# Projected keys copied out once, and their rows placed by transfers on chip

## The chip, the core and the metric

The kernel runs on one core of one Trainium2 chip. Its five engines each follow their own instruction list: TensorE (PE, matrix products; its weight loads are listed as PEld), VectorE (DVE), ScalarE (ACT), GpSimd (POOL) and SyncE (SP, which here issues nearly all transfers). [...]

The metric is the device time of one execution in microseconds. Three runs of the kernel before gave 834.16, 834.82 and 836.92 us; the median is 834.82 us.

## The reference, cut to what matters

One transformer block on 2048 tokens of width 512: adaptive layer norm, attention with 32 heads of 16 columns each, and a gated feed-forward part with 1792 inner columns.

```python
h = _layernorm(x) * (1 + ca) + sa
q, k, v = (h @ wqkv) split into 32 heads of 16
p = softmax(q @ k.T * 16 ** -0.5)        # per head, 2048 x 2048
x = x + ga * ((p @ v) @ wo)
h = _layernorm(x) * (1 + cb) + sb
x = x + gb * ((gelu(h @ w_gate) * (h @ w_up)) @ w_down)
```

The exponentials of the softmax are 32 x 2048 x 2048 numbers. The kernel handles them as 2048 tiles of 128 x 512.

## The kernel before, in words

**Heads and key buffers.** A block `dc` of 128 projected columns holds eight heads of 16 rows. The kernel works on four heads at a time, a head quad `qd` from 0 to 7: block `dc = qd // 2`, and in it the even heads (`ee = 0`) or the odd ones (`ee = 1`). Each of the four products of a quad takes a strip of 32 partitions, `32*j` to `32*j + 31`, which holds one even and one odd head. So that the product sees only one of the two, keys are stored twice: `km[0]` (`kme` in the profile) has the rows of the odd heads set to zero, and `km[1]` (`kmo`) those of the even heads. `side_k` makes them for one key group `g` of 512 tokens and one block `dc`: four products into the PSUM bank `mi`, then two VectorE instructions, each of which multiplies the whole bank by a column of zeros and ones (`self.rm`) and writes one of the two buffers.

**The stream of score tiles.** `stream()` goes through all tiles in order of position: quads 0 and 1 of the first 512 queries interleaved, then quads 2, 3 and on. For each step `qk()` puts two or three score tiles into one half of six PSUM banks, and one ScalarE instruction takes their exponential (line 336). Some rounds of four tiles are given to VectorE instead: four instructions turn scores into bits (line 348, `mreg<-ps_sc` and `dreg<-ps_sc`), and three more (`power_task`, lines 348 and 340) split and square them. Such a round is here called a vector round; it needs two free 2048-column buffers, keys and values that are marked as there, and a VectorE that the planner holds to be free soon.

**Who sets the order.** Nothing is scheduled at run time. While the program is built, `rec()` keeps a modelled clock for every engine and takes the next piece of work greedily: a score step, a product with values, a piece of side work, a vector round. What comes out is one fixed list per engine. `rec()` also finds each instruction's waits from the bytes that it reads and writes. One rule of it matters here: a transfer always waits, on its issuing engine, for the one before it on the same semaphore.

```python
if dma is not None and seq > 1:
    needs[stream] = seq - 1
```

The planner charges a transfer 450 ns of SP, and lets it land no earlier than 1.9 us after its issue began; the two masked key instructions are charged 661 ns each and a plain copy of the same bank 601 ns.

**Side work.** Projections for later quads are side work, spread over positions by `plan()`. `side_first` makes block 0 for key groups 1 to 3. Then `side_wo_load` clears `wo` on VectorE, waits until that is recorded, and issues eight transfers of 64 KB (`wo<-in_A_wo_dram`). After it come `side_dc(1)`, `side_mod`, `side_dc(2)`, `side_q_all(1)`, `side_dc(3)`; each `side_dc` makes the queries of a block and then, for the four key groups in turn, `side_k` and `side_v`. All share the one bank `mi`. As soon as the last product of `side_k` is planned, its key is marked as there (`self.done(("k", g, dc))`), and score steps and vector rounds may use it; the products then wait at their semaphores.

**What else SP issues.** After the loads of the prologue and `wo`, each finished quad gives a chain of eight transfers through DRAM for its softmax denominators (`unit_end`: `scr_den<-osb`, `den<-scr_den`, `scr_rec<-rden`, four times `rb<-scr_rec`). `rb` holds the reciprocals; GpSimd sets it to zero in the prologue, and until the last positions only rows `32*j` to `32*j + 15` of it are written.

## Time and profile before

| | |
|---|---|
| median of three runs | 834.82 us |
| the profiled execution: time, span | 834.12 us, 832.4 us |
| granted TensorE clock, mean | 0.994 |
| ACT busy | 799.0 us (96%) |
| PE busy | 744.3 us (89%) |
| DVE busy | 740.1 us (89%) |
| POOL busy | 4.5 us (1%) |
| score instructions on ScalarE | 716, 754.6 us |
| score tiles on VectorE | 400 (272 into `mreg`, 128 into `dreg`) |
| masked key instructions in `side_k` | 15 into `kme`, 15 into `kmo` |

The profiled execution is the program once, taken by the hardware profiler. Its span runs from the first to the last instruction; the remaining 1.7 us of its time lie around that. An engine that is busy 96% of the span is not thereby the bound in every stage, so the busy times are read by stage, and the chain of work that ended last is followed back. In the rows, `L318` is the line of the helper that records all matrix products, `L336` that of ScalarE instructions, `L348`, `L357` and `L340` those of the VectorE helpers, and `L386` that of transfers; the names behind the line (`kme<-ps_mi,rm`) tell the pieces apart. `SPq` is SP's queue issuing a transfer.

### The profile page before, as it was taken

The page shows a single profiled execution, that of the slowest core. Times are in us where ns is not written, and L with a number is a line of the kernel's source. Part 1 is how long each engine was busy: PE and PEld are TensorE (multiplying, and loading weights), DVE is VectorE, ACT ScalarE, POOL GpSimd, SP SyncE. Part 2 cuts the span into 40 slices and gives each one's busy share as a digit, 9 for nine tenths or more (in the row PEclk, how much of TensorE's full clock was granted, in tenths as well). Part 3 has the DMA queues.
Part 4 walks back from the last instruction along what each step waited for, and adds up shares of the span by engine and source line. Part 5 has one row for each costly group of instructions (what it writes and reads, how often), then busy time and mean ns, then how long its engine had stood idle before and what let it go on. Part 6 is the DMA issues. An engine that isn't in the chain of part 4 may idle for free.

```text
span 832.4 us, 29218 instructions
## 1 busy us (share of the span) xinstructions
PE 744.3 (89%) x13207; PEld 289.5 (35%) x13207; DVE 740.1 (89%) x1330; ACT 799.0 (96%) x754; POOL 4.5 (1%) x12
## 2 busy tenths in 40 slices
PE   8888989888898988899998989998889889898988
PEld 3333332322222221222333333333443344345556
DVE  7857999999999998999999999979999999597664
ACT  5999999999999999999999999999999999999982
POOL 2000000000000000000000000000000000000000
PEclk9999999999999999999999999999999999999999
DMA  9100000000003211110003212102462432500000
GB/s 287 43 23 16 9 10 9 10 9 8 9 9 90 59 46 34 46 34 22 23 6 96 64 48 56 54 26 59 139 182 62 135 93 70 152 13 7 20 7 13
DMA packets 76358, 43.68 MB, mean 52 GB/s; under 512 B 20557, under 2 KB 74634, under 8 KB 76234
## 3 DMA queue, kind: packets, MB, share of 16 engines
q1 hardware_dynamic: 76232, 41.82, 17.8%
q8 instruction: 103, 1.69, 0.8%
q14 instruction: 21, 0.17, 0.1%
q10 hardware_dynamic: 2, 0.00, 0.0%
HBM read 39.18 MB, written 2.61 MB: 50 GB/s over the span
## 4 chain that ended last, share of the span: by engine, by line
ACT 69%; PE 15%; DVE 10%; DMA 3%; SPq 1%; issue 1%; DVEq 0%
ACT E L336 66%; PE ps_sc L318 7%; PE ps_mi L318 6%; DVE mreg L348 3%; ACT hreg L336 2%; PE ps_pv L318 2%; DMA scr_rec<-rden 2%; DVE dreg L348 1%; SPq L386 1%; DMA rb<-scr_rec 1%; ACT L336 1%; DVE dreg L340 1%; DVE mreg L340 1%; DVE onorm L340 1%; DVE st L376 0%
## 5 line engine op out<-in xcount | busy, mean ns | idle before, releaser
L336 ACT ACTIVATE E<-ps_sc 128x1024 bf16<-128x1024 f32 (+2 forms) x716 | 754.6, 1263 | 19.0 <-PE ps_sc L318 18.6
L318 PE MATMUL ps_sc<-qT,kmo 32*128 32x256 bf16 (+2 forms) x1664 | 196.8, 299 | 23.6 <-ACT E L336 22.1
L318 PE MATMUL ps_sc<-qT,kme 32*128 32x256 bf16 (+2 forms) x1600 | 193.0, 306 | 25.2 <-ACT E L336 22.1
L348 DVE TENSOR_SCALAR mreg<-ps_sc 128x512 uint16<-128x512 f32 x272 | 182.3, 684 | 15.7 <-PE ps_sc L318 13.1
L318 PE MATMUL ps_pv<-E,vaug 128*17 128x256 bf16 (+2 forms) x2576 | 151.4, 300 | 2.2 <-DVE osb L357 1.5
L318 PE MATMUL ps_mi<-wreg,mreg 128*32 128x256 bf16 (+1 forms) x1856 | 108.4, 331 | 7.9 <-DVE hreg L340 3.1
L318 PEld LDWEIGHTS ps_sc<-qT,kme 32*128 32x128 bf16 x1600 | 53.1, 92 | 144.3 <-ACT E L336 119.1
L318 PEld LDWEIGHTS ps_sc<-qT,kmo 32*128 32x128 bf16 x1664 | 55.3, 92 | 130.4 <-ACT E L336 110.1
L348 DVE TENSOR_SCALAR dreg<-ps_sc 128x512 uint16<-128x512 f32 x128 | 85.8, 685 | 11.5 <-PE ps_sc L318 10.7
L318 PEld LDWEIGHTS ps_pv<-E,vaug 128*17 128x17 bf16 x2576 | 52.8, 89 | 58.9 <-issue 41.5
L348 DVE TENSOR_SCALAR mreg<-mreg 128x2048 uint16<-128x2048 uint16 x99 | 67.0, 682 | 0.2
L318 PEld LDWEIGHTS ps_mi<-wreg,mreg 128*32 128x32 bf16 x1856 | 41.5, 96 | 49.7 <-issue 21.0
L318 PE MATMUL ps_pv<-mreg,vaug 128*17 128x256 bf16 (+2 forms) x740 | 44.4, 304 | 5.9 <-DVE mreg L340 3.6
L340 DVE TENSOR_TENSOR dreg<-mreg,dreg 128x2048 bf16<-128x2048 bf16 x37 | 44.8, 1212 | 0.0
L318 PE MATMUL ps_mi<-hreg,wreg 128*32 128x512 bf16 x480 | 39.4, 385 | 1.3 <-DVE vaug L357 0.6
L340 DVE TENSOR_TENSOR mreg<-mreg 128x2048 bf16<-128x2048 bf16 x31 | 37.5, 1211 | 0.1
L340 DVE TENSOR_TENSOR hreg<-ps_mi,hreg 128x512 bf16<-128x512 f32 x46 | 31.5, 685 | 5.0 <-PE ps_mi L318 4.8
L357 DVE CAST hreg<-ps_mi 128x512 bf16<-128x512 f32 x46 | 31.5, 684 | 1.4 <-PE ps_mi L318 1.3
L318 PE MATMUL ps_pv<-dreg,vaug 128*17 128x256 bf16 (+2 forms) x508 | 31.1, 303 | 1.8 <-DVE dreg L340 1.4
L318 PE MATMUL ps_mi<-wo,onorm 128*32 128x512 bf16 x416 | 32.3, 384 | 0.1
L348 DVE TENSOR_SCALAR dreg<-dreg 128x2048 uint16<-128x2048 uint16 x44 | 30.0, 682 | 0.0
L318 PE MATMUL ps_mi<-mreg,hreg 128*32 128x512 bf16 x352 | 28.6, 384 | 0.0
(160 smaller groups left out, 668.4 us busy)
## 6 DMA issues: line engine op xcount, KB each, us to landing
mreg<-in_B_w_up_dram SPq DMA_DIRECT2D x32, 256.0 KB, 2.9
mreg<-in_B_w_gate_dram SPq DMA_DIRECT2D x28, 256.0 KB, 3.6
mreg<-in_B_w_down_dram SPq DMA_DIRECT2D x16, 256.0 KB, 2.7
dreg<-in_B_w_down_dram SPq DMA_DIRECT2D x12, 256.0 KB, 5.0
mreg<-in_w_mod_dram SPq DMA_DIRECT2D x1, 2048.0 KB, 12.1
rb<-scr_rec SPq DMA_DIRECT2D x64, 32.0 KB, 1.8
out_dram<-xs SPq DMA_DIRECT2D x16, 128.0 KB, 1.7
rb<-scr_rec SPq DMA_DIRECT2D x116, 16.0 KB, 1.7
```

The source lines that it names most:

```text
L318: return self.rec("pe", lambda e: e.matmul(out, lhsT, rhs, start=start, stop=stop, tile_position=tp), [lhsT, rhs, *after], [out], cost=(n, ...
L336: return self.rec("act", lambda e: e.activation(out, in_, func, scale=scale, **kw), rd, wr, cost=self.cost("act", out, [in_], "act") + load)
L340: return self.rec(eng, lambda e: e.tensor_tensor(out, a, b, op), [a, b], [out], cost=self.cost(eng, out, [a, b], "tt"))
L348: return self.rec(eng, lambda e: e.tensor_scalar(out, a, s1, s2, **kw), rd, [out], cost=self.cost(eng, out, [a], "ts") + (60 if len(rd) > ...
L357: return self.rec(eng, lambda e: e.tensor_copy(out, in_), [in_], [out], cost=self.cost(eng, out, [in_], "ts"))
L386: return e.dma_start(out, in_)
```

## The change

For block 0 nothing changes. For blocks 1 to 3 `side_k` copies the bank once, without a mask, into a new staging buffer `kst` (two halves, taken in turn by key groups), and then issues eight transfers from SP, one for each strip `j` and each of even and odd: 16 rows of 512 bf16, from `kst` into the rows of that head in `kme` or `kmo`. The rows of the other heads have to be zero, so a new function `zero_rows` issues 24 transfers, of 16 rows by 2048 columns, from rows of `rb` that stay zero into those rows of `kme` and `kmo`. It is called in `side_wo_load`, ahead of the loads of `wo`. The zero rows and the key rows of one strip in one of the two buffers share one semaphore, `dk0` to `dk7`.

```diff
@@ alloc
+        self.kst = sb("kst", [P, 2, 512], BF16)
@@ side_k
         def fin(mi):
-            self.ts("dve", self.km[0][:, dc, sl], mi, self.rm[:, 0:1], None, ALU.mult)
-            self.ts("dve", self.km[1][:, dc, sl], mi, self.rm[:, 1:2], None, ALU.mult)
+            if dc == 0:
+                self.ts("dve", self.km[0][:, dc, sl], mi, self.rm[:, 0:1], None, ALU.mult)
+                self.ts("dve", self.km[1][:, dc, sl], mi, self.rm[:, 1:2], None, ALU.mult)
+            else:
+                st = self.kst[:, g % 2, :]
+                self.copy("dve", st, mi)
+                for j in range(4):
+                    for ee in range(2):
+                        r = slice(32 * j + DH * ee, 32 * j + DH * ee + DH)
+                        self.dma("sp", self.km[ee][r, dc, sl], st[r, :], "dk%d" % (2 * j + ee))
             self.done(("k", g, dc))
         yield from self.side_proj(512 + P * dc, g, fin)
+
+    def zero_rows(self):
+
+        z = self.rb[:, :].bitcast(BF16)
+        for j in range(4):
+            for ee in range(2):
+                r = 32 * j + DH * (1 - ee)
+                for dc in range(1, NDC):
+                    self.dma("sp", self.km[ee][r:r + DH, dc, :], z[32 * j + DH:32 * j + 2 * DH, :], "dk%d" % (2 * j + ee))
@@ side_wo_load
         yield from self.until("wo0")
+        if not self.dry:
+            self.zero_rows()
         selv = self.self32[:, :].rearrange("p (a b) -> p a b", b=32)
```

## The prediction

> **What bounds the kernel now.** I read the page's busy times first, then the chain of work that ended last between 40 and 130 us, then the busy times by stretch.

> ```profile
> span 832.4 us, 29218 instructions
> PE 744.3 (89%) x13207; PEld 289.5 (35%) x13207; DVE 740.1 (89%) x1330; ACT 799.0 (96%) x754; POOL 4.5 (1%) x12
> ...
> 44.47 85.81 ACT E L336 x80
> ...
> core 0: us, PE busy (x) PEld busy (x) DVE busy (x) ACT busy (x) POOL busy (x), PEclk, DMA share, GB/s
> 55.00:85.00 30.00, 27.33 (x536) 10.19 (x532) 23.01 (x45) 30.00 (x29) 0.31 (x1) 1.00 0.11 26
> 85.00:165.00 80.00, 71.61 (x1286) 25.06 (x1282) 77.93 (x126) 80.00 (x76) 0.00 (x0) 1.00 0.04 10
> 165.00:330.00 165.00, 144.04 (x1724) 39.64 (x1724) 159.30 (x258) 163.87 (x153) 0.00 (x0) 0.99 0.12 33
> 700.00:832.00 132.00, 118.92 (x2607) 64.47 (x2603) 88.01 (x179) 111.91 (x115) 0.00 (x0) 0.99 0.14 35
> ```

> From 44.5 us on ScalarE does exponentials without a gap: 85.81 us of the chain are one piece of 80 instructions. The end therefore moves only in two ways: by the number of tiles that ScalarE has to do, or by a gap that it is given. VectorE takes tiles off it, and from 85 to 165 us it is itself full (77.93 of 80). From 55 to 85 us it isn't (23.01 of 30): there the first vector rounds wait for keys and values, not for VectorE.

> **The masked pair against the copy.** Twelve key evictions change, those of blocks 1 to 3. Of these, four lie in 55:85 and eight in 85:165.

> ```profile
> L348 DVE TENSOR_SCALAR kme<-ps_mi,rm 128x512 bf16<-128x512 f32 x15 | 11.2, 748 | 6.1 <-PE ps_mi L318 6.1
> L348 DVE TENSOR_SCALAR kmo<-ps_mi,rm 128x512 bf16<-128x512 f32 x15 | 11.1, 743 | 0.0
> ...
> 95.58 0.75 DVE L348 TENSOR_SCALAR kme<-ps_mi,rm 128x512 bf16<-128x512 f32 x1
> 96.25 0.74 DVE L348 TENSOR_SCALAR kmo<-ps_mi,rm 128x512 bf16<-128x512 f32 x1
> 96.91 1.42 DVE L340 TENSOR_TENSOR wo<-wo,ga 128x512 bf16<-128x512 bf16 x4
> 98.46 0.69 DVE L357 CAST vaug<-ps_mi 128x512 bf16<-128x512 f32 x1
> 99.07 0.68 DVE L348 TENSOR_SCALAR mreg<-ps_sc 128x512 uint16<-128x512 f32 x1
> ...
> 104.54 0.68 DVE L348 TENSOR_SCALAR mreg<-mreg 128x2048 uint16<-128x2048 uint16 x1
> 105.14 0.69 DVE L348 TENSOR_SCALAR dreg<-dreg 128x2048 uint16<-128x2048 uint16 x1
> ...
> 107.35 1.22 DVE L340 TENSOR_TENSOR mreg<-mreg 128x2048 bf16<-128x2048 bf16 x1
> 108.48 0.69 DVE L348 TENSOR_SCALAR mreg<-ps_sc 128x512 uint16<-128x512 f32 x1
> ...
> L336 ACT ACTIVATE E<-ps_sc 128x1024 bf16<-128x1024 f32 x47 | 46.0, 1164 | 0.0
> L336 ACT ACTIVATE E<-ps_sc 128x1536 bf16<-128x1536 f32 x29 | 41.6, 1576 | 0.0
> ```

> Durations overlap on VectorE, so I count from start to start. The pair takes 96.91 - 95.58 = 1.33 us. The nearest row to the copy, same bank and same output type, is the cast of `vaug`: 99.07 - 98.46 = 0.61. Saved: 0.72 us per eviction, 5.8 us for the eight where VectorE is full, 8.6 us for all twelve.

> What VectorE does with it: a vector round is four tiles at about 0.61 (the same pitch), two bit operations at 0.60 (105.14 - 104.54) and a square at 1.13 (108.48 - 107.35), 4.77 us or 1.19 per tile. ScalarE did 47 x 2 + 29 x 3 = 181 tiles in these 80 us, 0.44 per tile. When both are full, n tiles more on VectorE shorten the time by 0.44 n and fill 5.8 = (0.44 + 1.19) n, so n = 3.6 and the gain is 1.6 us. With all twelve it is 5.3 tiles and 2.3 us; with none taken, 0. I take 1.6, since only the full stretch turns time on VectorE into tiles. The bank `mi` also comes free 0.72 us sooner each time; PE, which reads it next, isn't the bound, so I count nothing.

> **The zero rows on SP.** 24 transfers of 64 KB, three to a semaphore, so two of each three wait on SP for the landing before: 16 waits. They need only `rb`, which is zero early, so they start when SP has issued the prologue's loads.

> ```profile
> 3.90 1.25 POOL L364 MEMSET rb<- 128x1024 f32 x1
> ...
> 12.63 1.40 SPq L386 DMA_DIRECT2D mreg<-in_w_mod_dram  x1
> 58.39 3.62 SPq L386 DMA_DIRECT2D wo<-in_A_wo_dram  x8
> 68.92 0.61 SPq L386 DMA_DIRECT2D scr_den<-osb  x1
> ...
> mreg<-in_w_mod_dram SPq DMA_DIRECT2D x1, 2048.0 KB, 12.1
> rb<-scr_rec SPq DMA_DIRECT2D x64, 32.0 KB, 1.8
> rb<-scr_rec SPq DMA_DIRECT2D x116, 16.0 KB, 1.7
> ...
> DMA to landing us min/median/max: 2.4/3.1/3.3
> ```

> SP is free from 14.03 to 58.39 us, and this is the cover. The first zero transfer lies behind the 2 MB of `w_mod`, which land at 12.63 + 12.1 = 24.7, so I let it land at 25.2. Then come 15 more waited landings and eight issues that nobody waits for (3.62 / 8 = 0.45 each). No row shows a transfer from SBUF to SBUF. The bounds are 1.8 us for a dependent step (16 to 32 KB into `rb`, 16 rows as here, 1.7 to 1.8) and 3.1 (the median of the `wo` loads, 64 KB, eight in a queue; last row); the first of those, alone, took 2.4. I take 2.3, nearest to that one. The end is 25.2 + 15 x 2.3 + 8 x 0.45 = 63.3 us; with 1.8 it is 55.8, with 3.1 it is 75.3.

> [...]

> **What stands behind it on SP.** The `wo` loads go from 58.39 to 63.3 and end at 66.9. Their reader, `wo<-wo,ga`, starts only at 94 us, so nothing is lost there. The keys of block 1 come next.

> ```profile
> 61.88 0.75 DVE L348 TENSOR_SCALAR kme<-ps_mi,rm 128x512 bf16<-128x512 f32 x1 [0.70 <-PE ps_mi L318]
> 62.55 0.74 DVE L348 TENSOR_SCALAR kmo<-ps_mi,rm 128x512 bf16<-128x512 f32 x1
> 72.56 0.74 DVE L348 TENSOR_SCALAR kme<-ps_mi,rm 128x512 bf16<-128x512 f32 x1
> ...
> 70.19 0.39 PE L318 MATMUL ps_sc<-qT,kmo 32*128 32x512 bf16 x3
> 71.61 0.39 PE L318 MATMUL ps_sc<-qT,kme 32*128 32x512 bf16 x2
> 72.47 0.39 PE L318 MATMUL ps_sc<-qT,kme 32*128 32x512 bf16 x3
> 77.10 0.39 PE L318 MATMUL ps_sc<-qT,kme 32*128 32x512 bf16 x3
> ```

> Today group 0 is complete at 63.3. Its first reader is the product at 71.61, the first on `kme` after the last block of quad 1. After the change the copy ends at 62.5, but SP issues from 66.9 to 70.5 (8 x 0.45), and each part lands 1.7 later: strip 0 of `kme` at 68.6, strip 1 at 69.5, strips 2 and 3 at 70.4 and 71.3. The readers come at 71.61 and 72.47, so 1.2 to 3 us are left: no stall. Each 0.1 us more per zero step takes 1.5 of that. Group 1's eight go from 70.5 to 74.1. Then the denominators of quad 0 are issued, 5 us later than their 68.92; quad 2, which needs their buffer, ends 30 us on, and that covers it. Group 2's copy (today at 72.56) needs the half of `kst` that group 0's transfers release at 72.2: free just in time. SP issues it from about 74.7 on; strip 2 lands at 74.7 + 4 x 0.45 + 1.7 = 78.2. Laid against the program's order, the third product at 77.10 is a vector round's tile on this group and strip: PE would stand 1.1 us, and ScalarE has part of one instruction in stock. With the copy perhaps held a little by `kst`, I charge 1.0 us for this stretch; bounds 0 (chain end 55.8) and 10 (below).

> For blocks 2 and 3 SP is idle but for denominators; a key is complete some 0.6 + 3.6 + 1.7 = 5.9 us after its products instead of 1.4. The nearest reader in block 2 comes at 107.19 for keys evicted at 95.58, in block 3 at 156 for 140.66, so 11 us or more cover it; without the cover each would cost up to 4.5.

> PE gets up to 96 waits on `dk` semaphores for 24 on VectorE. A row shows what it has in hand:

> ```profile
> L318 PEld LDWEIGHTS ps_sc<-qT,kme 32*128 32x128 bf16 x151 | 6.5, 91 | 20.0 <-ACT E L336 17.6 <-issue 1.7
> ```

> Between 55 and 165 us the weights of the `kme` products alone stood 17.6 us waiting for ScalarE; 72 waits more at an estimated 0.05 us (half of that row's 91 ns load) are 3.6 us and stay inside. I take 0, with 0 and 2 as bounds.

> **The sum.** 834.12 (the profiled execution, span 832.4 and 1.7 around it) - 1.6 + 1.0 = 833.5. The median of the runs is 0.7 above the profiled execution, so 834.2 for the median.

> **The rivals.** First, slower: the chain of zero rows is too long. It decides from 2.4 us a step on, where strip 3 lands after 72.47. At 2.6, between the least and the median of the `wo` row, the chain ends at 67.8, strip 2 lands at 74.9 against 72.47, and the loss is 2 us above the forecast's, so 836; at 3.1 it ends at 75.3, strip 0 lands at 80.6, and PE stands 9 us, with ScalarE behind it: 843. For it: 64 KB and queues in the `wo` row. Against it: no DRAM at either end, and nothing else in flight from 25 to 58 us.

> Second, slower: a new order. All that comes after 58 us is planned anew, since the planner sees other times. It pays at the end, where ScalarE is idle 20 of 132 us (700:832) because the last sets wait for each other. One vector round less is 4 x 0.44 = 1.8 us on ScalarE; two lost, or the wait of the last sets longer by as much, give 834.8 + 3.6 = 838.4. Against it: nothing in the profile says which way such a reshuffle falls.

> Third, faster: all twelve copies become tiles (-2.3), SP is in time (0), and the reshuffle brings a round (-1.8): 834.8 - 4.1 = 830.7. For it: VectorE is full in all stretches from 85 to 330. Against it: 55:85 has idle VectorE already.

> Fourth, the change saves VectorE time and no round takes it: 834.8 + 1.0 = 835.8. It falls in the same class as the forecast.

> **How the numbers follow.** 0.3% is 2.5 us, about what a measurement of this kernel tells from no change. Forecast and fourth rival together, 832.3 to 837.3: 0.37. First rival above that: 0.20. Second: 0.19. Third: 0.24. So faster 0.24, same 0.37, slower 0.39. The likeliest case's own range is 832.3 to 837.3. For eight in ten I leave out 0.07 below, where the third rival meets a second round gained (829.5), and 0.12 above, where the zero step passes 2.95 (842).

> **What would show it.** Right: 12 pairs gone, 12 casts into `kst` of 0.68; SP's zero rows from 14 to about 63 us, with steps of 2.3; the `wo` loads some 5 us later; no wait of a score product on a `kmo` or `kme` transfer over 1 us; 404 tiles on VectorE instead of 400. Wrong: ScalarE idle near 72 or 78 us (first rival); 396 tiles or fewer, or more than 20 us idle after 700 (second); 408 or more tiles (third).

## The result

The changed kernel takes 858.58 us (median of six runs, 855.46 to 861.94) against 835.87 for the kernel before (six runs beside them): a ratio of 1.0279, with a 95% interval of 1.0251 to 1.0308. It is 2.8% slower, and outside the predicted range. The profiled execution took 859.06 us.

The page of the changed kernel: span, busy times, the granted clock in 40 slices, and the score instructions (busy time, mean ns of one | idle time before them and who ended most of it; eight of the 713 belong to the feed-forward part at the end).

```profile
span 857.1 us, 29398 instructions
PE 759.3 (89%) x13217; PEld 291.8 (34%) x13223; DVE 734.2 (86%) x1318; ACT 802.5 (94%) x751; POOL 4.5 (1%) x12
...
PEclk9989799989999998999999999999999999999989
...
L336 ACT ACTIVATE E<-ps_sc 128x1024 bf16<-128x1024 f32 (+2 forms) x713 | 758.0, 1244 | 40.4 <-PE ps_sc L318 39.8
...
L348 DVE TENSOR_SCALAR mreg<-ps_sc 128x512 uint16<-128x512 f32 x252 | 169.2, 684 | 30.3 <-PE ps_sc L318 28.7
...
L348 DVE TENSOR_SCALAR dreg<-ps_sc 128x512 uint16<-128x512 f32 x148 | 99.1, 683 | 9.9 <-PE ps_sc L318 8.6
```

ScalarE has 3.5 us more to do (802.5 against 799.0) and stands idle 21.2 us more (span less busy: 54.6 against 33.4). VectorE does 252 + 148 = 400 tiles, as many as before. So no work was taken off ScalarE, and it was given gaps. Nearly all its idle time before score exponentials ends with a product of PE. The same stretches as in the prediction, and behind them short ones of 3.4 us:

```profile
core 0: us, PE busy (x) PEld busy (x) DVE busy (x) ACT busy (x) POOL busy (x), PEclk, DMA share, GB/s
55.00:85.00 30.00, 24.12 (x475) 9.08 (x471) 15.50 (x28) 26.21 (x25) 0.31 (x1) 1.00 0.21 44
85.00:165.00 80.00, 70.58 (x1131) 23.67 (x1131) 67.41 (x113) 71.10 (x65) 0.00 (x0) 0.91 0.09 21
...
38.65:42.05 3.40, 2.39 (x28) 1.01 (x30) 3.28 (x10) 3.40 (x4) 0.00 (x0) 1.00 0.27 42
42.05:45.45 3.40, 3.08 (x22) 0.71 (x26) 1.51 (x3) 1.92 (x3) 0.00 (x0) 0.50 0.33 54
...
83.00:86.40 3.40, 0.00 (x0) 0.00 (x0) 0.00 (x0) 0.00 (x0) 0.00 (x0) 1.00 0.10 26
86.40:89.80 3.40, 2.98 (x23) 0.67 (x27) 1.79 (x3) 1.02 (x1) 0.00 (x0) 0.50 0.09 20
89.80:93.20 3.40, 3.40 (x54) 1.35 (x54) 1.04 (x3) 2.46 (x2) 0.00 (x0) 0.50 0.07 17
...
127.40:130.80 3.40, 1.12 (x39) 0.48 (x27) 1.81 (x4) 1.71 (x3) 0.00 (x0) 1.00 0.10 22
130.80:134.20 3.40, 3.40 (x38) 0.62 (x26) 3.29 (x6) 2.66 (x3) 0.00 (x0) 0.50 0.12 29
```

ScalarE was full from 55 to 165 us; now it lacks 3.8 and 8.9 us there. From 83.0 to 86.4 no engine computes, and then the granted clock of PE is 0.50 for two stretches. The timelines of PE, ScalarE and VectorE name the two places (start, duration, engine, line, operation; in brackets the idle time before it and what ended it):

```profile
86.82 1.03 PE L318 MATMUL ps_sc<-qT,kme 32*128 32x512 bf16 x4 [5.13 <-DMA kme<-kst]
129.84 0.39 PE L318 MATMUL ps_pv<-dreg,vaug 128*17 128x512 bf16 x4 [2.28 <-DVE dreg L348]
...
87.89 1.02 ACT L336 ACTIVATE E<-ps_sc 128x1024 bf16<-128x1024 f32 x1 [4.98 <-PE ps_sc L318]
...
77.62 0.69 DVE L357 CAST kst<-ps_mi 128x512 bf16<-128x512 f32 x1 [3.17 <-DMA kmo<-kst]
...
128.99 0.25 DVE L360 RECIPROCAL rden<-den 128x16 f32<-128x16 f32 x1 [2.54 <-DMA den<-scr_den]
```

The first place is the product of a vector round that stands on a key of block 1 still on its way: PE waits 5.13 us for `kme<-kst`, and ScalarE behind it 4.98. The second is of another kind. VectorE's list holds the reciprocal of the denominators, and this waits 2.54 us for `den<-scr_den`. A tile of `dreg` stands behind it, and a product with values behind that, so PE stands 2.28 us. At 179.38 the same happens once more (2.24 us). SP's timeline shows why the keys and the denominators came late:

```profile
60.59 5.09 SPq L386 DMA_DIRECT2D kmo<-rb  x3
65.72 4.52 SPq L386 DMA_DIRECT2D wo<-in_A_wo_dram  x8
70.36 0.51 SPq L386 DMA_DIRECT2D kme<-kst  x1
...
71.55 1.61 SPq L386 DMA_DIRECT2D kme<-kst  x1
...
76.41 0.53 SPq L386 DMA_DIRECT2D kme<-kst  x1
...
84.96 0.59 SPq L386 DMA_DIRECT2D kme<-kst  x1
...
120.43 0.53 SPq L386 DMA_DIRECT2D scr_den<-osb  x1
121.06 0.55 SPq L386 DMA_DIRECT2D kme<-kst  x1
...
127.07 0.58 SPq L386 DMA_DIRECT2D den<-scr_den  x1
```

The zero rows end at 65.7, the `wo` loads at 70.2, and group 0 takes SP from 70.36 to 76.41: 6.05 us for eight, not 3.6. Group 1 takes 5.4, one transfer of denominators follows at 81.78, group 2 begins at 82.48, and its fifth transfer, strip 2 of `kme`, is issued at 84.96 and lands at 86.8. Each takes 0.63 us of SP from start to start, a few nearly a us more (71.55). At 120 us eight key transfers stand between the two halves of a denominator's way through DRAM: 6.64 us from `scr_den<-osb` to `den<-scr_den`, where the kernel before has 1.70 on its SP:

```profile
125.84 0.50 SPq L386 DMA_DIRECT2D scr_den<-osb  x1
127.54 0.33 SPq L386 DMA_DIRECT2D den<-scr_den  x1
```

Where the 24.7 us between the two profiled executions arose, counted by when each had done so many of its 2048 score tiles (ends of the exponentials and of VectorE's tiles in the traces; us later than before; e1 to f1 are the runs below):

```
tiles done (us, before)   after      e1      e2      e3      e5      n2      c3      d3      f1
120 (69.1)                 +2.4    +1.8    -1.2    +1.5    -0.4    +2.1    -0.3    +2.8    -1.0
160 (85.4)                +11.5    +5.9    -1.7    +1.5    +7.5    +2.1    +0.3    +2.2    -1.4
200 (99.4)                +13.1    +7.1    -0.8    +2.4   +10.1    +2.1    +4.5    +3.0    +0.8
260 (121.2)               +16.5    +5.4    -2.5    +2.4    +9.8    +2.5    +3.9    +1.3    -0.5
400 (172.7)               +18.3    +8.1    -3.7    +2.1    +8.0    +1.7    +3.2    +0.1    -2.1
1000 (391.3)              +21.9   +14.1    -1.4    +1.0    +9.1    +2.9    +4.8    +1.4    -1.5
1700 (657.7)              +24.2   +12.8    +4.5    +0.8    +9.1    +6.2    +5.4    +2.7    -0.1
2048 (806.7)              +24.7   +14.5    +7.7    +1.0   +12.3    +7.4    +5.1    +5.1    -3.3
```

9.1 us come between tiles 120 and 160 (late keys and the half clock behind them), 1.6 up to tile 200 (a stretch of half clock at 103.5, with PE busy 2.85 of the 3.40 us ahead of it), 3.4 up to tile 260 (the late reciprocal at 129 and its half clock, 0.50 in 130.80:134.20), 1.8 up to 400 (the one at 179). The last 6.4 come where none of the change's transfers run any more. The first 2.4 follow two stretches of half clock, from 42.05 to 48.85 us, ahead of every key transfer; I come back to it at the end.

### The profile page after: what moved, and what is told of

It is laid out like the page before. It is cut to its first block, busy times and chain, and to the rows that moved or that the text cites. A ratio compares the mean times of both kernels' runs of the same rounds, so it can differ in the third digit from the quotient of the medians.

```text
span 857.1 us, 29398 instructions
## 1 busy us (share of the span) xinstructions
PE 759.3 (89%) x13217; PEld 291.8 (34%) x13223; DVE 734.2 (86%) x1318; ACT 802.5 (94%) x751; POOL 4.5 (1%) x12
## 4 chain that ended last, share of the span: by engine, by line
ACT 65%; PE 18%; DVE 9%; SPq 4%; DMA 4%; issue 1%; DVEq 0%
ACT E L336 60%; PE ps_sc L318 9%; PE ps_mi L318 6%; SPq L386 4%; PE ps_pv L318 3%; ACT hreg L336 3%; DVE mreg L348 2%; DVE dreg L348 2%; ACT L336 1%; DMA rb<-scr_rec 1%; DMA den<-scr_den 1%; DVE mreg L340 1%; DVE wreg L340 1%; DVE xs L340 1%; DVE osb L357 0%
## 5 line engine op out<-in xcount | busy, mean ns | idle before, releaser
L336 ACT ACTIVATE E<-ps_sc 128x1024 bf16<-128x1024 f32 (+2 forms) x713 | 758.0, 1244 | 40.4 <-PE ps_sc L318 39.8
L318 PE MATMUL ps_sc<-qT,kme 32*128 32x256 bf16 (+2 forms) x1600 | 204.1, 312 | 30.8 <-ACT E L336 22.3
L318 PE MATMUL ps_sc<-qT,kmo 32*128 32x256 bf16 (+2 forms) x1664 | 199.3, 303 | 25.9 <-ACT E L336 23.2
L348 DVE TENSOR_SCALAR mreg<-ps_sc 128x512 uint16<-128x512 f32 x252 | 169.2, 684 | 30.3 <-PE ps_sc L318 28.7
L318 PE MATMUL ps_pv<-E,vaug 128*17 128x256 bf16 (+2 forms) x2564 | 155.2, 305 | 1.8 <-DVE osb L357 1.1
L318 PE MATMUL ps_mi<-wreg,mreg 128*32 128x256 bf16 (+1 forms) x1888 | 109.7, 330 | 8.1 <-DVE hreg L340 4.3
L348 DVE TENSOR_SCALAR dreg<-ps_sc 128x512 uint16<-128x512 f32 x148 | 99.1, 683 | 9.9 <-PE ps_sc L318 8.6
L318 PEld LDWEIGHTS ps_sc<-qT,kme 32*128 32x128 bf16 x1600 | 54.9, 92 | 149.7 <-ACT E L336 113.3
L318 PEld LDWEIGHTS ps_sc<-qT,kmo 32*128 32x128 bf16 x1664 | 56.1, 92 | 138.7 <-ACT E L336 112.0
L318 PEld LDWEIGHTS ps_pv<-E,vaug 128*17 128x17 bf16 x2564 | 53.0, 90 | 60.9 <-issue 44.1
L348 DVE TENSOR_SCALAR mreg<-mreg 128x2048 uint16<-128x2048 uint16 x103 | 69.6, 682 | 0.2
L318 PEld LDWEIGHTS ps_mi<-wreg,mreg 128*32 128x32 bf16 x1888 | 41.2, 95 | 51.5 <-issue 20.7
L318 PE MATMUL ps_pv<-mreg,vaug 128*17 128x256 bf16 (+2 forms) x756 | 47.0, 309 | 4.5 <-DVE mreg L340 3.4
L340 DVE TENSOR_TENSOR mreg<-mreg 128x2048 bf16<-128x2048 bf16 x40 | 48.5, 1213 | 0.1
L318 PE MATMUL ps_mi<-hreg,wreg 128*32 128x512 bf16 x480 | 43.2, 415 | 1.0 <-DVE hreg L348 0.4
L340 DVE TENSOR_TENSOR hreg<-ps_mi,hreg 128x512 bf16<-128x512 f32 x47 | 32.1, 683 | 5.0 <-PE ps_mi L318 4.6
L348 DVE TENSOR_SCALAR dreg<-dreg 128x2048 uint16<-128x2048 uint16 x53 | 36.1, 680 | 0.1
L318 PE MATMUL ps_mi<-wo,onorm 128*32 128x512 bf16 x416 | 32.2, 388 | 1.7 <-DVE wreg L340 0.7
L357 DVE CAST hreg<-ps_mi 128x512 bf16<-128x512 f32 x45 | 30.8, 684 | 3.1 <-PE ps_mi L318 2.8
L318 PE MATMUL ps_pv<-dreg,vaug 128*17 128x256 bf16 (+2 forms) x508 | 28.9, 293 | 4.4 <-DVE dreg L348 3.4
L318 PE MATMUL ps_sc<-xs,ident 128*32 128x512 bf16 x276 | 23.7, 403 | 10.1 <-ACT E L336 9.8
L318 PE MATMUL ps_mi<-mreg,hreg 128*32 128x512 bf16 x352 | 29.6, 385 | 0.0
## 6 DMA issues: line engine op xcount, KB each, us to landing
mreg<-in_w_mod_dram SPq DMA_DIRECT2D x1, 2048.0 KB, 11.7
```

Of the source, the lines that this page charges most:

```text
L318: return self.rec("pe", lambda e: e.matmul(out, lhsT, rhs, start=start, stop=stop, tile_position=tp), [lhsT, rhs, *after], [out], cost=(n, ...
L336: return self.rec("act", lambda e: e.activation(out, in_, func, scale=scale, **kw), rd, wr, cost=self.cost("act", out, [in_], "act") + load)
L340: return self.rec(eng, lambda e: e.tensor_tensor(out, a, b, op), [a, b], [out], cost=self.cost(eng, out, [a, b], "tt"))
L348: return self.rec(eng, lambda e: e.tensor_scalar(out, a, s1, s2, **kw), rd, [out], cost=self.cost(eng, out, [a], "ts") + (60 if len(rd) > ...
L357: return self.rec(eng, lambda e: e.tensor_copy(out, in_), [in_], [out], cost=self.cost(eng, out, [in_], "ts"))
```

## The experiments

Three theories were laid against each other: that the transfers come late (keys first, then denominators), that the new order of the instructions costs it, and that the copy saves nothing. All ratios are against runs of the kernel before on the same chip (832.8 to 834.4 us). `L348` and `L357` stand five lines lower in the kernels that change the planner's model of a transfer.

**The chain of zero rows.** Each zero transfer of the changed kernel gets a semaphore of its own, so that SP waits for none of them:

```diff
-                    self.dma("sp", self.km[ee][r:r + DH, dc, :], z[...], "dk%d" % (2 * j + ee))
+                    self.dma("sp", self.km[ee][r:r + DH, dc, :], z[...], "dz%d%d" % (2 * j + ee, dc))
```

> The changed kernel, but each of the 24 zero transfers has a semaphore of its own, so SP issues them without a wait (24 x about 0.6 us, from 14 to some 30 us) and is free long before the keys of block 1. Theory A (keys of block 1 come late because SP is still busy with the chain, its 16 waited landings): the 5.1 us wait at 86.8 us and the low-clock stretches behind it go, and the time comes back to 832 to 839 us. Rival B (a key that goes through eight transfers is complete some 6 us after its products, chain or not, and PE waits for it at many places): 845 to 858 us, with waits of score products for kme<-kst or kmo<-kst left in blocks 1 to 3.

848.06 us, ratio 1.018 [1.0146, 1.0214]: 1.0% back of 2.8. PE still waits 3.07 us for `kme<-kst`, now at 79.91, and VectorE's reciprocal 3.21 us at 170.0. The time is that of the rival, though only one such wait of PE is left. The chain's lateness is a part, and no more.

The chain alone, put in the kernel before at the same place: 24 transfers of 16 rows by 1024 columns into a buffer that nobody reads, three to a semaphore (`kdum` for `km[ee]`, called in `side_wo_load`). PE, VectorE and ScalarE keep their lists.

> The kernel before, masked keys and all, with 24 chained zero transfers (16 rows by 1024 columns here) into a buffer that nobody reads, at the same place in SP's list. The lists of PE, VectorE and ScalarE are the same as before. Theory A: a late SP harms only through the keys, so within 0.3% of before. Rival: the chain harms by itself (late wo loads, late denominators, traffic): slower by 1% or more.

832.86 us, 1.0012 [0.9978, 1.0046]. The traffic of the chain and its 24 issues cost nothing by themselves. With rows half as long it ends at 59.3 here, ahead of the `wo` loads (59.93), so nothing behind it came late in this run. That late `wo` loads do no harm is read from the changed kernel: issued from 65.72 on, they have landed by 72.8, and their first reader, `wo<-wo,ga`, starts at 106.0.

**What one stand of PE costs.** In the kernel before, one product of quad 2 is made to wait for two dependent transfers of 64 bytes; its order is untouched:

```diff
+        after = ()
+        if not self.held_once and items[0][0][0][1] == 2 and items[0][0][1] == 4:
+            self.held_once = True
+            after = self.hold()   # two 64-byte transfers, each after the last
...
-                        self.qT[...], tp=(32 * j, 0))
+                        self.qT[...], tp=(32 * j, 0), after=after)
```

> The kernel before with the same lists on PE, VectorE and ScalarE, and one hold that the planner does not know of: the first score product of quad 2 in round 4 (about 78 us) waits for two transfers of 64 bytes, one after the other, of which the first reads a ScalarE result of that moment; some 3 to 5 us of PE standing. Clock theory: PE standing for most of a 3.4 us stretch halves the granted clock for the next one or two, so the loss is the gap on ScalarE plus 2 us or more, with a half-clock stretch right behind it. Rival: the loss is the gap alone, 2 to 4 us, and the clock stays.

841.14 us, 1.0102 [1.0072, 1.0133]: 8.4 us for one wait. Its timelines, and three stretches of 3.4 us:

```profile
82.72 0.61 PE L318 MATMUL ps_sc<-qT,kme 32*128 32x512 bf16 x3 [4.80 <-DMA dum<-dum]
...
83.37 1.02 ACT L336 ACTIVATE E<-ps_sc 128x1024 bf16<-128x1024 f32 x1 [4.19 <-PE ps_sc L318]
```

```profile
79.10:82.50 3.40, 0.00 (x0) 0.00 (x0) 0.00 (x0) 0.08 (x1) 0.00 (x0) 1.00 0.06 12
82.50:85.90 3.40, 3.18 (x73) 1.89 (x73) 1.41 (x3) 2.04 (x2) 0.00 (x0) 0.50 0.02 5
85.90:89.30 3.40, 3.40 (x29) 0.73 (x30) 3.19 (x9) 2.85 (x4) 0.00 (x0) 0.50 0.03 2
```

PE stood 4.80 us and ScalarE 4.19, and then the granted clock was 0.50 for 6.8 us, in which and just behind which ScalarE waited for it four times more (1.4 us in sum). In the traces the kernel is 0.8 us ahead of before at tile 140 and 4.9 behind at tile 160, a loss of 5.7; the remaining 2 to 3 us of the medians I can't place. So this stand of PE cost 1.2 to 1.75 times its 4.80 us, and I put the 9.1 us between tiles 120 and 160 of the changed kernel down to its stand of 5.13, the two stretches at half clock, and VectorE's wait of 3.17 at 77.62 before them.

**The copy alone.** The kernel before, with one copy into `km[0]` for blocks 1 to 3 and both quads' products reading it. The zeroing of the other head's rows is left out, and so are all transfers:

```diff
+                self.copy("dve", self.km[0][:, dc, sl], mi)
...
-                        self.km[ee][32 * j:32 * j + 32, dc, P * kt:P * kt + P],
+                        self.km[ee if dc == 0 else 0][32 * j:32 * j + 32, dc, P * kt:P * kt + P],
```

> The kernel before, but the keys of blocks 1 to 3 are copied once, without a mask, into kme, and both parities read kme; no transfers, no kst, no zero rows (the rows of the other head are not zeroed, so the scores of blocks 1 to 3 mix two heads). It measures the saved VectorE time by itself. By the prediction's term: 1.6 us faster (0 to 2.3), 0.2%, with 404 score tiles on VectorE. Rival: the planner turns it into nothing or a worse order: within 2 us of before or up to 4 us slower.

846.85 us, 1.0174 [1.014, 1.0208]: without one of the transfers, still 1.7% slower. VectorE's groups:

```profile
L348 DVE TENSOR_SCALAR mreg<-ps_sc 128x512 uint16<-128x512 f32 x264 | 176.9, 686 | 22.8 <-PE ps_sc L318 21.4
...
L348 DVE TENSOR_SCALAR dreg<-ps_sc 128x512 uint16<-128x512 f32 x140 | 94.4, 686 | 15.8 <-PE ps_sc L318 14.8
```

264 + 140 = 404 tiles, the forecast number. The table above has it 1.2 us ahead of before at tile 120, a lead that it has from tile 60 on, ahead of its first copy, and 3.7 at tile 400: 2.5 us gained. The saving is there. It is lost later, most of it behind tile 1000, in stretches of low clock (0.7 to 0.8 on its page between 717 and 738 us, where the kernel before has 0.9 or more) and, behind the last tile, one wait of ScalarE of 5.8 us for `st`; no copy runs there, and what differs is the order that the planner found.

**Another order of the same work.** So the kernel before was run twice with one constant of the planner's model a little higher. The instructions stay the same, and only their order differs:

```diff
-            return n * 0.833 + (57 if ps else 92)
+            return n * 0.833 + (58 if ps else 92)    # n1: ScalarE from PSUM
...
-        return n * 1.042 / f + 68
+        return n * 1.042 / f + 70                    # n2: VectorE
```

> The kernel before with one constant of the planner's charge for a ScalarE instruction on PSUM raised from 57 to 58 ns. Work, tiling and transfers are the same; only the order that the planner finds differs. Theory C (what is left of the loss without the chain, 1.8%, and the loss of the copy alone, 1.7%, is that of a new order, any new order): slower by 0.7 to 2.5%, with a mean granted clock of 0.97 to 0.985 and more half-clock stretches than before. Rival D (the loss belongs to the copy and the transfers): within 0.4% of before.

> The kernel before with one constant of the planner's charge for a VectorE instruction raised from 68 to 70 ns; the same work in another order. Theory C: slower by 0.7 to 3%, clock 0.965 to 0.985. Rival D: within 0.4% of before.

840.31 us, 1.0087 [1.0053, 1.0122], and 841.0, 1.01 [1.0061, 1.0138]. A change that does nothing but shuffle costs this kernel 0.9 to 1.0%, twice out of two. The granted clock goes with it: its mean is 0.985 in the profiled execution of each, 0.994 in that of the kernel before. The same two constants under the copy alone:

> The copy alone (keys of blocks 1 to 3 copied once into kme, read by both parities, the other head's rows not zeroed), in the order that the planner finds with 58 for 57 ns at ScalarE. To be set against the kernel before with the same constant (0.9% slower than before). Theory C (the copy by itself saves some 2 to 3 us, and its 1.7% loss was its order): 832 to 842 us, at or under that kernel's 840.3. Rival D (the copy itself costs 1.7%): 846 us or more.

> The copy alone, in the order found with 70 for 68 ns at VectorE; to be set against the kernel before with that constant (1.0% slower than before, 841.0). Theory C: 830 to 840 us. Rival D: 846 us or more.

836.1 us, 1.0039 [1.001, 1.0069], and 833.98, 1.0005 [0.9981, 1.0029]. At equal constants the copy is 0.5 and 0.95% faster than the masked pair; at the constants that both kernels came with (e2) it is 1.7% slower. The spread between orders is larger than the saving, so its size in us can't be told from three pairs. What n1, n2 and e2 agree on is that the order of the kernel before is a better one than its neighbours.

**Vector rounds only on keys that have landed.** The changed kernel, chain kept, where a vector round may take a key only after its last transfer has landed by the planner's clock:

```diff
+                    self.land[("k", g, dc)] = op.t1
...
-                          and all(k in self.have for k in self.keys(seq[rounds[cand[0]][2]]))):
+                          and all(k in self.have and self.land.get(k, 0) <= t for k in self.keys(seq[rounds[cand[0]][2]]))):
```

> The changed kernel, chain included, but a vector round is opened only on keys whose transfers have landed by the planner's clock. Theory A for the place of the direct loss: the 5.1 us in which PE stood at 86.8 us was the tile of a vector round opened on keys in flight, so that gap falls below 1.5 us; the rest of the order's loss stays: 842 to 852 us. Rival: the gap belongs to score products that come in their turn; it stays at 3 us or more: 853 to 860 us.

848.37 us, 1.0188 [1.015, 1.0225]. The wait of 5.13 us is gone; left are 2.06 at 73.03, a product in its turn, and 0.39 behind it. In time this gives back as much as e1 did. At the place itself it gives back little: three stretches of half clock follow (the page has the clock at 0.7 to 0.8 between 63.4 and 84.5 us), and 7.9 us are lost between tiles 120 and 160 where the changed kernel lost 9.1. Most of its gain comes later, where its order is another one too.

Both together, with two other constants:

> The whole change with zero transfers on semaphores of their own and vector rounds only on landed keys, in the order found with 70 for 68 ns at VectorE. Theory C with A: as the copy alone with that constant, plus what is left of late keys, 0 to 3 us: 831 to 843. Rival B (transfers cost at many places): 846 us or more, with waits of score products for kst transfers over 3 us in sum.

> As the last, with the planner's constants as they were but for its charge for a semaphore between engines, 50 in place of 60 ns. Theory C: another order, 828 to 843 us; where it falls in that range is not to be told beforehand. Rival B: 846 us or more.

841.64 us, 1.0139 [1.0086, 1.0191] with 70 for VectorE, and 844.29, 1.0152 [1.0114, 1.0189] with 50 instead of 60 ns for a semaphore. No product waits for keys any more: c3 loses 0.6 us between tiles 120 and 160, where the changed kernel lost 9.1. Yet both lie above n1 and n2, the kernel before in other orders. In the first, timelines of VectorE, PE, ScalarE and SP:

```profile
89.17 0.25 DVE L360 RECIPROCAL rden<-den 128x16 f32<-128x16 f32 x1 [3.15 <-DMA den<-scr_den]
...
90.02 0.39 PE L318 MATMUL ps_sc<-qT,kmo 32*128 32x512 bf16 x1 [2.06 <-DVE mreg L348]
...
91.73 1.94 ACT L336 ACTIVATE E<-ps_sc 128x1024 bf16<-128x1024 f32 x2 [2.37 <-PE ps_sc L318]
...
80.24 0.55 SPq L386 DMA_DIRECT2D scr_den<-osb  x1
...
87.39 0.58 SPq L386 DMA_DIRECT2D den<-scr_den  x1
```

This is the second place of the changed kernel again: eight key transfers between the halves of the denominators' way, a reciprocal that holds VectorE 3.15 us, PE 2.06 behind it, ScalarE 2.37 behind that. By the table this place costs c3 3.6 us (from +0.3 at tile 160 to +3.9 at 260). The planner, which charges SP 450 ns a transfer where it takes 630, put the reciprocal too early. In c4 the same waits are 3.65 at 90.3 and 2.27 at 174.1.

**Telling the planner, or taking SP out of it.** First, own semaphores and landed keys, and the measured cost of these transfers in the planner's model; then the same with another constant for VectorE (72):

```diff
+            if op.tag:     # key and zero transfers on chip
+                self.free[eng] = t + 630
+                op.t1 = max(t + 650, self.dma_free) + 1000 + size / 105
+                return
```

> The whole change with own semaphores for the zero rows and vector rounds on landed keys, and the planner told what a transfer on chip costs: SP 630 ns in place of 450, landing about 1.8 us after the issue began. Theory E (the denominators' transfers stand behind the key transfers on SP; the planner takes them for landed, so the reciprocal holds VectorE's list for 2 to 4 us, and then PE): no wait of a reciprocal for den over 1.5 us between 60 and 190 us, 832 to 842 us. Rival B (the transfers hold PE themselves): 844 us or more, with PE standing on kme or kmo transfers.

> As the last, in the order found with 72 for 68 ns at VectorE. Theory E: the same absence of long reciprocal waits, 830 to 842 us; rival B: 844 us or more.

837.86 us, 1.0048 [1.0023, 1.0072], and 836.1, 1.0045 [1.0023, 1.0068]. In the first the waits for `den` sum to 1.3 us over three, but the last step of the same way is late instead, and ScalarE has a gap of 2.01 us at 95.45 behind it:

```profile
92.74 0.69 DVE L345 TENSOR_TENSOR onorm<-osb,rb 128x512 bf16<-128x512 f32 x1 [2.11 <-DMA rb<-scr_rec]
```

In the second the reciprocal still waits 2.90 us at 91.66, against what was expected, with a gap of 2.25 on ScalarE behind it; that its time is no longer than d1's shows how much else an order moves.

Second, c3 with the odd heads' transfers issued by GpSimd, so that SP has four of each eight:

```diff
-                        op = self.dma("sp", self.km[ee][r, dc, sl], st[r, :], "dk%d" % (2 * j + ee))
+                        op = self.dma(("sp", "pool")[ee], self.km[ee][r, dc, sl], st[r, :], "dk%d" % (2 * j + ee))
```

> To be set against the run with the whole change in the order of 70 ns at VectorE (841.6 us, a reciprocal wait of 3.15 us at 89 us): the four transfers of the odd heads are issued by GpSimd, which has nothing else to do, so SP spends half the time on keys. Theory E: the denominators' transfers come 2.5 us earlier per key group, the long reciprocal wait goes or falls under 1 us, and the time comes to 832 to 839 us. Rival B: no change, 840 to 844 us.

835.92 us, 1.0038 [1.0013, 1.0063]: 1.0% less than c3, and the intervals don't meet. SP and VectorE at the place where c3 stood:

```profile
79.31 0.55 SPq L386 DMA_DIRECT2D scr_den<-osb  x1
80.38 2.43 SPq L386 DMA_DIRECT2D kme<-kst  x4
82.85 0.58 SPq L386 DMA_DIRECT2D den<-scr_den  x1
...
85.36 0.25 DVE L360 RECIPROCAL rden<-den 128x16 f32<-128x16 f32 x1
```

Four transfers between the halves instead of eight, 3.54 us instead of 7.15, and the reciprocal finds its numbers there. The waits for denominators sum to 0.9 us, ScalarE gets no gap of over 1 us between 60 and 200, and the ratio is below n2's, which is the kernel before at the same constant. In the table the place costs nothing: 2.2 us behind before at tile 160, 1.3 at tile 260, where c3 goes from 0.3 to 3.9. (The execution profiled, 839.54 us, is the slowest of this run's ten; its page has the clock at 0.7 to 0.8 between 712 and 733 us.)

**Zeros by GpSimd in the prologue.** The changed kernel without `zero_rows`; GpSimd clears `km[ee][:, 1:NDC, :]` by two memsets instead, and `FILL`, the PE work that the planner keeps in any 3.4 us, is 4400 instead of 4200.

> The changed kernel with the zero rows made by two GpSimd memsets of kme and kmo in the prologue in place of the 24 transfers, and the planner's target for TensorE work in each 3.4 us stretch raised from 4200 to 4400 columns (it places more idle products). Theory C: the change by itself is worth 1.6 us or a little more, and a denser order keeps the clock up: 824 to 836 us, clock 0.985 or more. Rival B (late keys at many places): 845 us or more.

848.74 us, 1.018 [1.0143, 1.0217]. The expectation failed for a reason of its own. The start comes 8.6 us late (at tile 60); GpSimd and VectorE, timelines:

```profile
5.09 5.21 POOL L364 MEMSET kme<- 128x6144 bf16 x1
10.25 5.21 POOL L364 MEMSET kmo<- 128x6144 bf16 x1
...
5.52 9.97 DVE L348 TENSOR_SCALAR sc_bf<-tcol 128x4 bf16<-128x4 f32 x1
5.60 9.89 DVE L376 BATCH_NORM_STATS2 st<-xs 128x6 f32<-128x512 bf16 x1
```

A small `tensor_scalar` on VectorE, 0.17 us in the kernel before, lasts 9.97 and ends at 15.49, when the memsets end (15.46); the instruction behind it, 0.69 us elsewhere, ends with it. Of late keys the run shows that they don't need the chain: with no zero transfer on SP, PE still stands 2.88 us for `kme<-kst` at 86.51.

**The best version.** GpSimd for the odd heads, the told planner, own semaphores, landed keys and `FILL` 4400; then with `FILL` 4600 and 58 for ScalarE; then with `FILL` 4400, 64 for VectorE and 56 for ScalarE.

> Odd keys issued by GpSimd, planner told the cost of transfers on chip, and its target for TensorE work raised from 4200 to 4400 columns per 3.4 us. Theory E with C: 828 to 838 us, clock 0.985 or more. Rival B: 842 us or more.

> Odd keys issued by GpSimd, own semaphores for the zero rows, vector rounds on landed keys, planner told the cost of transfers on chip; constants 4600 for 4200 columns of TensorE work and 58 for 57 ns at ScalarE. If the copy's saving (2 to 3 us) is left once the late keys, the late denominators and a poor order are mended: 827 to 832 us, 0.2 to 0.7% under before. If an order of before's quality can't be had so: 832 to 838 us.

> As the last with 4400 columns, 64 for 68 ns at VectorE and 56 for 57 ns at ScalarE. The same two cases: 827 to 832 us, or 832 to 838 us.

833.7 us, 1.001 [0.9986, 1.0034]; 830.08, 0.9958 [0.9931, 0.9985]; 835.43, 1.0021 [0.9995, 1.0048]. The second, the fastest of these three, is 0.4% faster than the kernel before. Its page:

```profile
span 829.0 us, 29737 instructions
PE 752.4 (91%) x13363; PEld 292.1 (35%) x13363; DVE 742.6 (90%) x1332; ACT 795.8 (96%) x753; POOL 28.3 (3%) x60
...
L353 DVE TENSOR_SCALAR mreg<-ps_sc 128x512 uint16<-128x512 f32 x264 | 177.3, 684 | 14.3 <-PE ps_sc L323 11.2
...
L353 DVE TENSOR_SCALAR dreg<-ps_sc 128x512 uint16<-128x512 f32 x144 | 96.8, 684 | 5.7 <-PE ps_sc L323 4.1
```

408 tiles on VectorE, and ScalarE has 3.2 us less to do than in the kernel before. How much of the 0.4% belongs to the copy and how much to this order, one of three tried, stays open: the kernel before wasn't run with `FILL` 4600.

## Why the prediction was wrong

The forecast 834.2 us, no change, was wrong, and so was its range. In the trace the 24.7 us are 9.1 at late keys, 5.2 at late denominators, 6.4 later on, where only the order differs, and 2.4 and 1.6 at the half clock from 42.05 and from 103.5 on, which neither explains. The runs bear out the first three in kind: with the chain's waits off SP, or the rounds later, the ratio falls from 2.8 to 1.8 and 1.9% (e1, e5), with both 1.4 and 1.5 are left (c3, c4), with the denominators relieved 0.4 to 0.5 (d1 to d3); and a mere reordering costs 0.9 and 1.0% (n1, n2). Against these stands the copy's saving. Each of these kernels is planned anew, so the sizes are rough, and the step from c3 and c4 to d1 to d3 in particular holds the luck of five orders beside the denominators.

By the prediction's steps:

- **The copy, right in kind, not taken.** Twelve casts of 688 ns came. The 404 tiles came in the copy alone, with 2.5 us gained between tiles 120 and 400 (c1 and c2: 1.7 each), where 1.6 was taken and 2.3 the bound. In the changed kernel VectorE stood at its new waits and did 400.
- **The zero step, nearly right.** Twelve of the fifteen dependent steps took 2.24 to 2.50 us, the others 2.7, 2.8 and 3.4; the mean is 2.44, forecast 2.3. The chain ends at 65.7 and not 63.3: 2.1 us come from the steps and 0.8 from the issues that nobody waits for (0.55 each, not 0.45), less 0.5 for an earlier start. The first rival's 2.6 was too high by about as much as 2.3 was too low; the row of the `wo` minimum, 2.4, was nearest.
- **"SP issues (8 x 0.45)", wrong in size.** The row that gave 0.45 is of loads from DRAM. The key transfers between buffers on chip took 0.63 each from start to start, and 8 of the 96 took 1.3 to 1.6. Landings of 1.7 were right (median 1.8, longest 3.7). This and the chain's end moved strip 2 of group 2 from 78.2 to 86.8: 2.4 us from the chain, 1.0 from `wo`, 2.45 and 1.8 from groups 0 and 1, 0.8 within group 2, and 0.1 from the denominators' transfer ahead of it.
- **"I charge 1.0 us for this stretch; bounds 0 … and 10", wrong.** The place was right: the third product at 77.10, a vector round on this group and strip. With every issue at its measured size the same working has strip 2 land at 86.8, 9.7 us after that product. PE came to it 4.6 us later than in the kernel before (at 81.69), delayed by the half clock at 42 us and by waits on the way, and stood 5.13 us. Group 2's copy, "perhaps held a little by `kst`", was held 3.17 us. What the working left out is the half clock behind such a stand (e4: 4.80 us of stand, 5.7 to 8.4 of loss).
- **"Quad 2, which needs their buffer, ends 30 us on, and that covers it", the step that failed in kind.** It asked who needs the buffer next and not who reads the data first. The first reader is the reciprocal, in VectorE's list at a fixed place. The late one of the prediction's own case, at 87.50 on SP, did no harm; those at 127 and 177 us did. (A late reciprocal isn't always dear: one waits 3.52 us at 511.88, long after the last key transfer, while ScalarE is busy with the feed-forward part, and ScalarE gets no gap.) And "SP is idle but for denominators" in blocks 2 and 3 counts SP's time, while the denominators' two halves can stand either side of eight issues of 0.63.
- **Blocks 2 and 3, right for the keys.** After 87 us no product waits for `kst`; the 11 us cover.
- **The new order, right in kind, mis-sized.** 838.4 with 0.19 was the second rival. Its price was drawn from vector rounds, 1.8 us each; n1 and n2 lose two rounds and one (392 and 396 tiles), 3.5 and 1.8 us at that price, but 5.9 and 6.6 us in time. No row of one trace can show that its order is a lucky one, but that constants of a planner stand at odd values (57, 68) and that everything behind 58 us is planned anew were both in view, and 0.19 was too little.

The first rival named the right place (PE at late keys) but hung it on the zero step, with 2.4 us as the point from which it decides. The mean step came out at that point, 2.44, but gave only 2.4 of the 8.6 us by which strip 2 came late; nearly all of the rest is SP's issue time, which decided.

## What to carry to other kernels

When transfers are added to a queue, ask of every transfer behind them which instruction reads it first and what stands behind that instruction in its engine's fixed list; a buffer that comes free much later is no cover. Price the issue by a row of the same kind of transfer, and tell a static planner that price before letting it plan around them. And in a kernel whose fixed order may be a lucky or a tuned one, run two neutral reorderings first: here they cost 0.9 and 1.0%, more than the change could save.

## What the runs showed of the hardware that was not expected

```profile
38.65:42.05 3.40, 2.40 (x30) 1.06 (x32) 3.20 (x9) 3.40 (x5) 0.00 (x0) 1.00 0.24 39
42.05:45.45 3.40, 2.86 (x77) 1.18 (x69) 1.41 (x2) 2.96 (x4) 0.00 (x0) 1.00 0.34 54
```

The kernel before and c3, with these same lists, did 2.39 and 2.40 us there and kept theirs too; e1 and e3, with 2.53 and 2.40, lost it a little later (mean clock 0.85 and 0.81 in 42.05:45.45, then 0.65 and 0.69 in 45.45:48.90). So the first 2.4 us of the table aren't laid to the change. What decides it stays open.

The key transfers from buffer to buffer on chip took 0.63 us of SP each in the changed kernel, back to back, against 0.45 for the `wo` loads from DRAM in the kernel before, and now and then nearly a us more (71.55 above). In d3 and f1 GpSimd issued half of them without a wait seen to follow; they landed in a median of 2.7 us in d3 where SP's took 2.1, and in f1 both took 2.1 to 2.2.

In b1 a VectorE `tensor_scalar` of 0.17 us lasted 9.97 us beside two GpSimd memsets of 5.21 us in a row, and ended 0.03 us behind the second. The cause isn't shown. In the kernel before nothing lasted longer beside the memset of `rb` (3.90 to 5.15), but no such instruction stood beside it: the `tensor_scalar` came at 5.60, and the BATCH_NORM_STATS2 that ran beside it took its usual 0.69. A `tensor_scalar` of a single column beside the memset of `vaug` (at 2.56) took 0.15, so not every one was lengthened.
